# Half of a causal convolution, for the last 2 x 256 tokens, on GpSimd and VectorE instead of TensorE

## The chip, the core and the metric

The kernel runs on one core of a Trainium2 chip. The core has a matrix engine (TensorE, PE in the profile; its weight loads are PEld), three engines for elementwise work (VectorE, DVE; ScalarE, ACT; GpSimd, POOL), and SyncE (SP), which here only issues transfers. Each engine runs its own instructions in the order in which they were issued; between engines, semaphores order the work. TensorE writes only to PSUM, the accumulator memory of eight banks; everything else lies in SBUF, both with 128 partitions. The metric is the device time of one execution in microseconds, median of several runs.

## The reference

The reference computes a retention layer (attention with a fixed decay and no softmax), then a gated linear unit whose gate is a causal convolution of five taps, each channel with its own weights:

```python
scores = q @ k.T / sqrt(64)
x = (scores * gamma[h] ** (i - j), zero for j > i) @ v      # (8, 8, 576, 64) -> (8, 576, 512)
for t in range(5):
    gate_pre += conv_w[t] * xp[:, t:t + 576, :]             # xp: x with four zero tokens in front
out = (sigmoid(gate_pre) * (x @ w_val)) @ w_out
```

Inputs and output are float32; there are 8 batches, 8 heads of 64 channels, and 576 tokens in each batch. The convolution works along the tokens, channel by channel.

## The kernel before

**Units and jobs.** The 576 tokens of a batch are two chunks of 256 and a rest of 64. A chunk is a *unit* of work for the retention; the rests of four batches together make a unit too. There are 18 units: 0 to 15 are chunks, 16 and 17 (`"tail"`) hold the leftover tokens of batches 0 to 3 and 4 to 7, 256 columns each. The gated linear unit works in *jobs*: jobs 0 to 3 are one unit each, jobs 4 to 9 two units, jobs 10 and 11 (`LAST - 1` and `LAST`) are units 16 and 17.

**One unit.** The keys, queries and values are loaded (`load_half`), cast to bf16 (`cast_half`, mostly on GpSimd), turned by TensorE (`turn_bank`), multiplied (`scores`), masked on VectorE (`masks`) and applied to the values, with a carried state for the earlier chunks (`carried`, `values`, `update`, `states`). `take_x` then multiplies the result by the query side of the decay and writes it, bf16, into `xg`. This tile holds x for all tokens as channels (128 partitions x 4 blocks) by tokens, with four zero columns in front of each batch, so that a tap of the convolution is a shifted view of it: `xs(j, rows, blk, shift)`.

**One job.** `conv` does the convolution on TensorE as matmuls with diagonal matrices: `dg` holds, for each block of 128 channels and each tap, a 64x64 diagonal of weights, made from the table `cw` (one column per tap and block) in `prep_conv`. For each pair of blocks (a *set*: blocks 0 and 1, or 2 and 3) it takes 5 taps x 4 quarters = 20 matmuls, and the second block of a set comes out with its two halves of 64 partitions exchanged. `gates` takes the sigmoid of it on ScalarE from PSUM to SBUF (L585; L581 for the last job). `value` is the product with `w_val`, 4 matmuls per block, and `gated` multiplies the two on VectorE into `z` or `zz` (L608). `project` multiplies by `w_out`, for the even and odd tokens of a unit apart (r = 0, 1), ScalarE copies the result into `big` (L623), and `store` sends it out by transfers issued on SP. The last job has its own end: two value products (L940) with their products on VectorE (L941), then `last_rows`, which projects job 11 into the PSUM tiles `s`, `a` and `v`, copies them with ScalarE and VectorE (L638 to L640) and issues the last stores.

**PSUM tiles.** `a`, `s` and the two `o` tiles have one buffer each, `v` has two. A new use of such a tile waits until the last reader of the use before is done. So the order of the readers on ScalarE and VectorE decides when TensorE may go on.

**Order.** There is no planner: the calls in the program are the order on every engine. All work around the change is in the lines behind the loop over the units (L894 to L942): for n = 16 it finishes units 16 and 17, then alternates the convs and value products of jobs 10 and 11 with the projections of units 14, 15 and 16 (`rows_out`), and ends with `last_rows`. Every helper that issues a matmul does so by one wrapper, so all matmuls carry line 169, and the tile names tell them apart: `a<-xg,dg` or `s<-xg,dg` is a conv, `v<-xg,wvb` a value product, `<-wob` a projection.

Of the kernel before, what the change touches and what calls it, by code (L numbers as in the profile page):

```python
# [13 lines left out]
F32 = mybir.dt.float32  # L14
BF16 = mybir.dt.bfloat16
AF = mybir.ActivationFunctionType
ALU = mybir.AluOpType
# [4 lines left out]
def kernel(  # L22
# [10 lines left out]
    nc = tc.nc  # L33
    B, H, S, D = q.shape
    DM = moe_w_val.shape[0]
    KC = moe_conv_w.shape[0]
    P = 128
    NP = H // 2
    NCH = S // P
    TAIL = S - NCH * P  # L40
# [3 lines left out]
    W = 2 * P  # L44
# [7 lines left out]
    ldp = ctx.enter_context(tc.tile_pool(name="ld", bufs=2))  # L52
# [22 lines left out]
    LAST = len(jobs) - 1  # L75
    HALVED = 3
    lo, hi = slice(0, 64), slice(64, 128)
# [3 lines left out]
    with tc.manual_schedule():  # L81
# [52 lines left out]
        taps = moe_conv_w.rearrange("k (o i) -> (k o) i", i=P)  # L134
# [112 lines left out]
        wob = consts.tile([P, NP, DM], BF16, name="wob")  # L247
        dg = consts.tile([P, NP, KC, 64], BF16, name="dg")

        def prep_conv():  # L250
            n = KC * NP
            cps = ps_a.tile([P, 2 * n + 4], F32, name="a")
            twice = cwn.rearrange("p e i -> p (e i)")
            transpose(cps[:, 0:n], twice[:, 0:P], identf[0:n, 0:n])
            transpose(cps[:, n + 1:2 * n + 1], twice[:, 64:192], identf[0:n, 0:n])
            cw = small.tile([P, n], F32, name="cw")
            nc.vector.tensor_copy(cw.rearrange("p (m e) -> p m e", e=2),
                                  cps.rearrange("p (e m two) -> p m e two", e=2, two=2)[:, 0:n // 2, :, 0])
            nc.vector.tensor_tensor(
                dg.rearrange("p o k j -> p k o j"),  # L260
                cw.rearrange("p (k o) -> p k o", o=NP).unsqueeze(3).to_broadcast([P, KC, NP, 64]),
                id2.unsqueeze(1).unsqueeze(1).to_broadcast([P, KC, NP, 64]), op=ALU.mult)
# [69 lines left out]
        def turn_bank(u, hf, ps, take=True):  # L332
            for i in range(2):
                for prl in range(2):
                    for r in range(2):
                        h = 2 * (2 * hf + prl)
                        transpose(ps[:, i, prl, r, :], bf[u]["kq"[i]][:, r, h:h + 2, :].rearrange("p h d -> p (h d)"), ident)
            if take:
                take_bank(u, hf, ps)

        def take_bank(u, hf, ps, eng=None):
            new_turned(u)
            (eng or nc.scalar.copy)(kqt[u][hf].rearrange("p i l r c a -> p (i l r c a)"), ps.rearrange("p i l r a -> p (i l r a)"))  # L343
# [9 lines left out]
        def turn_halves(*pairs, pool=None):  # L353
            if len(pairs) == 1 and pool is None:
                turn_bank(*pairs[0], ps_v.tile([P, 2, 2, 2, P], BF16, name="v"))
            else:
                ps = ps_a.tile([P, 2, 2, 2, 2, P], BF16, name="a")
                for (at, pair) in enumerate(pairs):
                    turn_bank(*pair, ps[:, at], take=False)
                for (at, pair) in enumerate(pairs):  # L360
                    take_bank(*pair, ps[:, at])
# [105 lines left out]
        def take_x(u, cs=(0, 1)):  # L467
            kind, b, cu = units[u]
            x = xg
            o = ops[u]  # L470
            for c in cs:
                if kind == "full":
                    i0 = (2 * cu + c) * P
                    nc.vector.tensor_tensor(  # L474
                        x[:, b, :, PAD + i0:PAD + i0 + P].rearrange("p o (a r) -> p o r a", r=2),
                        o[c].rearrange("p o (r a) -> p o r a", r=2),
                        gout[:, :, i0:i0 + P].rearrange("p o (r a) -> p o r a", r=2), op=ALU.mult)
                else:
                    i0 = NC2 * W
                    for i in range(2):  # L480
                        nc.vector.tensor_tensor(
                            x[:, b + 2 * c + i, :, PAD + i0:PAD + S].rearrange("p o (a r) -> p o r a", r=2),
                            o[c].rearrange("p o (r a) -> p o r a", r=2)[:, :, :, i * 32:i * 32 + 32],
                            gout[:, :, i0:S].rearrange("p o (r a) -> p o r a", r=2), op=ALU.mult)
# [58 lines left out]
        def width(j):  # L543
            return W * len(jobs[j])

        def xs(j, rows, blk, shift):
            kind, b, c = units[jobs[j][0]]
            if kind == "full":
                c0 = c * W + shift
                return xg[rows, b, blk, c0:c0 + width(j)]  # L550
            c0 = NC2 * W + shift
            return xg[rows, b:b + GB * len(jobs[j]), blk, c0:c0 + TAIL]

        gsb, zsb = {}, {}
# [3 lines left out]
        def sets(j, i):  # L558
            return (0, 1) if len(jobs[j]) == 1 and j != HALVED else (i,)

        cps = {}

        def conv(j, i, gate=True, pool=None):
            n, ss = width(j), sets(j, i)
            g = (pool or ps_a).tile([P, 2, 2 * W], F32, name="s" if pool else "a").rearrange("p e (s n) -> p e s n", n=n)[:, :, 0:len(ss)]
            for si, s in enumerate(ss):
                a, b = 2 * s, 2 * s + 1
                for kk in range(KC):
                    for (rows, blk, cols, bank) in ((lo, a, lo, 0), (hi, a, hi, 0), (lo, b, hi, 1), (hi, b, lo, 1)):
                        matmul(g[cols, bank, si, :], lhsT=dg[rows, blk, kk, :], rhs=xs(j, rows, blk, kk),  # L570
                                         start=(si == 0 and kk == 0), stop=(si == len(ss) - 1 and kk == KC - 1),
                                         skip_group_check=True)
            cps[j, i] = g
            if gate:
                gates(j, i)

        def gates(j, i):
            if j == LAST:
                t = [gp.tile([P, 1, len(sets(j, i)), width(j)], F32, name=f"last{e}", bufs=1) for e in range(2)]
                for e in range(2):  # L580
                    nc.scalar.activation(t[e], cps[j, i][:, e:e + 1], AF.Sigmoid)  # L581
                t = [t[e][:, 0] for e in range(2)]
            else:
                t = gp.tile([P, 2, 2 * W], F32, name="gate").rearrange("p e (s n) -> p e s n", n=width(j))[:, :, 0:len(sets(j, i))]
                nc.scalar.activation(t, cps[j, i], AF.Sigmoid)  # L585
                t = [t[:, e] for e in range(2)]
            gsb[j, i] = t
            if i == 0:
                if len(jobs[j]) == 1:
                    zsb[j] = zp.tile([P, NP, width(j)], BF16, name="z", bufs=4)  # L590
                else:
                    zsb[j] = zp.tile([P, NP, width(j)], BF16, name="zz", bufs=2)
# [54 lines left out]
        def stores(n):  # L647
            for u in waiting[:n]:
                store(u)
            del waiting[:n]  # L650

        def store(u):
            kind, b, c = units[u]
            ob = outs[u]
            if kind == "full":
                nc.sync.dma_start(out=out[b, c * W:(c + 1) * W, :].rearrange("(p r) n -> p r n", r=2), in_=ob)
            else:
                for i in range(GB):
                    nc.sync.dma_start(out=out[b + i, NC2 * W:S, :].rearrange("(p r) n -> p r n", r=2),
                                      in_=ob[i * 32:(i + 1) * 32])  # L660
# [3 lines left out]
        def gate_values(j, i, e):  # L664
            value(j, i, e)
            gated(j, i, e)
# [167 lines left out]
        for n in range(4, NU - 2):  # L834
# [4 lines left out]
            j, i = (HALVED, n - 4) if n < 6 else place[n - 2 - n % 2][0:1] + (n % 2,)  # L839
# [54 lines left out]
        n = NU - 2  # L894
        stores(2)
        j = place[n - 1][0]

        def rows_out(u, pools):
            for r in range(2):
                project(*place[u], r, pool=pools[r])  # L900
            waiting.append(u)
            stores(2)
# [10 lines left out]
        scores(n + 1, 0)  # L913
        masks(n + 1, 0)
        turn_halves((n + 1, 1), pool=ps_a)
        rows_out(n - 3, (None, None))
        scores(n + 1, 1, lambda: carried(n + 1, 1), pool=ps_a)
        masks(n + 1, 1)
# [7 lines left out]
        conv(LAST - 1, 0)  # L926
        gated(j, 1, 1)
        take_x(n + 1)
        stores(2)
        rows_out(n - 2, (ps_s, None))  # L930
        gate_values(LAST - 1, 0, 0)
        gate_values(LAST - 1, 0, 1)
        conv(LAST, 0)
        rows_out(n - 1, (ps_s, ps_o))
        gate_values(LAST, 0, 0)
        rows_out(n, (ps_s, ps_o))
        vp = [ps_v.tile([P, W], F32, name="v") for b in range(2)]
        for b in range(2):
# [34 lines left out]
```

## Time and profile before

| | us |
|---|---|
| median of three runs (lowest, highest) | 156.22 (156.05, 157.23) |
| the profiled execution's own time | 156.97 |
| its span, from the first to the last instruction or transfer | 155.3 |
| busy: TensorE / VectorE / ScalarE / GpSimd | 141.3 / 106.3 / 94.5 / 103.2 |
| granted clock of TensorE, mean | 0.999 |

The engines' own times at the end, from the timeline: the tokens of unit 16 are gathered by VectorE at 130.10 to 131.59 us from the start (`take_x`, L481), those of unit 17 at 137.39 to 138.87; the conv of job 10 is on TensorE from 136.68 us on, that of job 11 from 141.51 us; `last_rows` begins at 147.97 and the last copy out of PSUM ends at 150.55. The stores land by 155.3.

Durations in the profile are those of one execution. A "group" in it is all instructions of one line, engine, operation and shape: how many, their busy time, the mean of one in nanoseconds, and how long the engine sat idle before them, with what ended that. "128x512 bf16<-128x512 f32" gives output and input as partitions x elements. The "chain that ended last" goes back from the last instruction to what released it, step by step. "issue" is time in which the engine waited for nothing that the profile shows.

### The profile page before, as it was taken

Reading aid. Unit: us, or ns where it says so; the run is one execution under the profiler, and the core shown is the slowest. Engines: PE = TensorE matmul, PEld = TensorE weight load, DVE = VectorE, ACT = ScalarE, POOL = GpSimd, SP = SyncE. Lnnn points to the kernel's source line nnn. Section 1 sums busy time; section 2 is a strip of 40 time slices with the busy share of each in tenths; the row PEclk is TensorE's granted clock in tenths of the full one; section 3 lists DMA queues with packets and bytes.
Section 4 is the critical chain, followed back from the end, with each engine's and each line's share of the span. In section 5 each row is a group of like instructions: output and inputs, shape, how many; then the busy total and the mean of one; then the engine's idle time right before and its main releaser. Section 6 shows DMA issues by size and latency. Waiting matters only on the chain.

```text
span 155.3 us, 7164 instructions
## 1 busy us (share of the span) xinstructions
PE 141.3 (91%) x3054; PEld 89.9 (58%) x3054; DVE 106.3 (68%) x222; ACT 94.5 (61%) x161; POOL 103.2 (66%) x167
## 2 busy tenths in 40 slices
PE   6877979989698999899999999999999999999960
PEld 2356666878547465656565665647565645557530
DVE  4877785598686568587968796776778678653130
ACT  6995747585676775656567676766665544533530
POOL 7878788879998949794978789697869371000000
PEclk9999999999999999999999999999999999999999
DMA  4999999999999777789878997999979828995355
GB/s 111 347 347 342 313 313 294 332 301 344 275 306 269 209 252 231 223 235 304 258 210 226 303 293 215 283 292 272 214 243 248 231 48 324 412 412 220 133 141 135
DMA packets 62194, 40.60 MB, mean 261 GB/s; under 512 B 3498, under 2 KB 58834, under 8 KB 62162
## 3 DMA queue, kind: packets, MB, share of 16 engines
q1 hardware_dynamic: 61488, 39.59, 83.9%
q10 hardware_dynamic: 674, 0.55, 1.3%
q8 instruction: 24, 0.39, 1.1%
q14 instruction: 8, 0.07, 0.1%
HBM read 30.43 MB, written 9.44 MB: 257 GB/s over the span
## 4 chain that ended last, share of the span: by engine, by line
PE 68%; SPq 10%; DMA 8%; POOL 4%; ACT 3%; issue 3%; DVE 1%; POOLq 0%; ACTq 0%; DVEq 0%
PE v L169 35%; PE a L169 18%; PE s L169 8%; PE o L169 7%; DMA fk<-in_k_dram 5%; SPq L98 4%; DMA fq<-in_moe_w_val_dram 3%; SPq L121 3%; SPq L150 2%; ACT wvb L268 1%; POOL vb L290 1%; ACT gate L585 1%; DVE z L608 1%; POOL qb L297 1%; POOL s L530 0%
## 5 line engine op out<-in xcount | busy, mean ns | idle before, releaser
L169 PE MATMUL v<-xg,wvb 128*128 128x256 bf16 (+1 forms) x192 | 35.2, 326 | 0.2 <-ACT wvb L268 0.2
L343 ACT COPY kq<-a 128x1024 bf16<-128x1024 bf16 x25 | 25.3, 1012 | 16.6 <-PE a L169 15.9
L290 POOL TENSOR_TENSOR vb<-fv,gin 128x512 bf16<-128x512 f32 x32 | 32.7, 1042 | 3.2 <-DMA fv<-in_v_dram 3.2
L608 DVE TENSOR_TENSOR zz<-gate,v 128x512 bf16<-128x512 f32 x24 | 16.5, 687 | 15.1 <-PE v L169 12.4
L585 ACT ACTIVATE gate<-a 128x1024 f32<-128x1024 f32 (+1 forms) x17 | 16.5, 973 | 15.5 <-PE a L169 15.5
L398 DVE TENSOR_TENSOR p<-s,mask 128x1024 bf16<-128x1024 f32 x16 | 19.5, 1220 | 7.8 <-PE s L169 7.8
L169 PEld LDWEIGHTS <-wvb 128*128 128x128 bf16 x192 | 17.6, 97 | 11.8 <-issue 1.0
L474 DVE TENSOR_TENSOR xg<-o,gout 128x512 bf16<-128x512 f32 x32 | 22.3, 737 | 2.2 <-PE o L169 2.2
L169 PE MATMUL a<-xg,dg 64*64 64x256 bf16 (+1 forms) x460 | 21.7, 321 | 0.3 <-DVE xg L474 0.3
L297 POOL CAST kb<-fk 128x512 bf16<-128x512 f32 x32 | 19.7, 617 | 2.6 <-DMA fk<-in_k_dram 2.0
L623 ACT COPY big<-v 128x512 f32<-128x512 f32 x29 | 16.9, 581 | 6.2 <-PE v L169 6.0
L169 PE MATMUL v<-wob,zz 128*128 128x512 bf16 x84 | 20.1, 379 | 0.0
L169 PEld LDWEIGHTS <-kb 64*64 64x64 bf16 (+1 forms) x652 | 14.7, 106 | 8.3 <-DVE p L398 0.9
L297 POOL CAST qb<-fq 128x512 bf16<-128x512 f32 x26 | 15.9, 613 | 3.2 <-DMA fq<-in_q_dram 3.1
L394 DVE TENSOR_TENSOR p<-v,mask 128x512 bf16<-128x512 f32 x26 | 16.7, 683 | 0.5
L169 PEld LDWEIGHTS <-kq 64*64 64x64 bf16 x576 | 11.3, 106 | 9.5 <-issue 8.1
L169 PEld LDWEIGHTS <-dg 64*64 64x64 bf16 x480 | 12.8, 106 | 4.6 <-issue 0.7
L169 PEld LDWEIGHTS <-zz 128*128 128x128 bf16 x96 | 8.8, 98 | 9.5 <-issue 0.7
L169 PE MATMUL o<-p,vb 64*64 64x128 bf16 x576 | 13.1, 218 | 0.8 <-issue 0.4
L169 PE MATMUL o<-kq,s 64*64 64x128 bf16 (+1 forms) x256 | 11.2, 212 | 0.6 <-issue 0.5
L169 PEld LDWEIGHTS <-vb 64*64 64x64 bf16 x576 | 10.0, 107 | 2.5 <-issue 2.4
L608 DVE TENSOR_TENSOR z<-gate,v 128x512 bf16<-128x512 f32 (+1 forms) x12 | 7.0, 589 | 6.0 <-PE v L169 5.8
(108 smaller groups left out, 210.5 us busy)
## 6 DMA issues: line engine op xcount, KB each, us to landing
out_dram<-big SPq DMA_DIRECT2D x16, 512.0 KB, 5.9
fk<-in_k_dram SPq DMA_DIRECT2D x28, 256.0 KB, 4.7
fq<-in_q_dram SPq DMA_DIRECT2D x28, 256.0 KB, 4.8
fv<-in_v_dram SPq DMA_DIRECT2D x27, 256.0 KB, 4.6
big<-in_k_dram SPq DMA_DIRECT2D x2, 512.0 KB, 5.0
big<-in_q_dram SPq DMA_DIRECT2D x2, 512.0 KB, 5.5
big<-in_v_dram SPq DMA_DIRECT2D x2, 512.0 KB, 5.9
big<-in_moe_w_out_dram SPq DMA_DIRECT2D x4, 256.0 KB, 4.8
```

What stands on the lines that cost most here:

```text
L98: nc.sync.dma_start(out=t, in_=src[b, :, c * W:(c + 1) * W, :].rearrange("h (p r) d -> p h (r d)", r=2))
L121: queue.dma_start(out=t[:, hs], in_=SRC[n][b, hs, c * W:(c + 1) * W, :].rearrange("h (p r) d -> p h (r d)", r=2))
L169: return f(*a, **k)
L290: nc.gpsimd.tensor_tensor(b[n][:, hs].rearrange("p h r d -> p (h r) d"), f.rearrange("p h (r d) -> p (h r) d", r=2), gin[:, units[u][2], h ...
L297: (eng or nc.gpsimd.tensor_copy)(b[n][:, :, hs].rearrange("p r h d -> p h r d"), f.rearrange("p h (r d) -> p h r d", r=2))
L343: (eng or nc.scalar.copy)(kqt[u][hf].rearrange("p i l r c a -> p (i l r c a)"), ps.rearrange("p i l r a -> p (i l r a)"))
L394: nc.vector.tensor_tensor(p[:, par].rearrange("p l r a -> p l (r a)"), sps[u, hf][par].rearrange("p l r a -> p l (r a)"), mrow.to_broadcas ...
L398: nc.vector.tensor_tensor(p.rearrange("p e l r a -> p (e l) (r a)"), sps[u, hf].rearrange("p e l r a -> p (e l) (r a)"), mrow.to_broadcast ...
L474: nc.vector.tensor_tensor(x[:, b, :, PAD + i0:PAD + i0 + P].rearrange("p o (a r) -> p o r a", r=2), o[c].rearrange("p o (r a) -> p o r a", ...
L585: nc.scalar.activation(t, cps[j, i], AF.Sigmoid)
L608: nc.vector.tensor_tensor(zsb[j][:, 2 * e + ss[0]:2 * e + ss[-1] + 1, :], gsb[j, i][e], vps[j, i, e], op=ALU.mult)
L623: (eng or nc.scalar.copy)(outs[u][:, r], o)
```

## The change

For jobs 10 and 11 alone, TensorE's `conv` does only the first set (blocks 0 and 1). Blocks 2 and 3 are computed from the same `xg` by a new function, `conv_off`, in float32:

- Block 2 on GpSimd. Five instructions multiply the shifted views by their column of `cw`, the first into the job's sum, the others into four parts of a scratch tile; three additions bring these together.
- Block 3 on VectorE. One such product, then four instructions that each multiply a view by its weight and add it to the sum.

The sums lie in one tile (`fq`, four parts of 256 columns: two jobs, two blocks) and the scratch in another (`fk`); these are the buffers into which queries and keys were loaded before. `gates_off` takes the sigmoid of the sums on ScalarE, from SBUF, into the second half of the gate tiles. For block 3 it is two instructions, which exchange the halves of 64 partitions as the matmuls did. The sigmoids that read PSUM take only the first set.

In the order of the calls, GpSimd's part for job 10 stands right after the turning of unit 17; VectorE's for job 10 and GpSimd's for job 11 after `take_x` of unit 17; VectorE's for job 11 after the last product of job 10 with its gate. Matmuls of `value`, `project` and `last_rows` stay as they are.

```diff
+            taken.append(cw)                                   # in prep_conv
...
+        OFF = (LAST - 1, LAST)
+
+        def conv_off(j, e, eng):
+            if not pre:
+                free = [ldp.tile([P, H, 2 * D], F32, name=nm).rearrange("p h d -> p (h d)").rearrange("p (t n) -> p t n", n=W)
+                        for nm in ("fk", "fq")]
+                for at, jj in enumerate(OFF):
+                    pre[jj] = free[1][:, 2 * at:2 * at + 2]
+                pre["taps"] = free[0]
+            acc = pre[j][:, e]
+            for kk in range(KC):
+                w = taken[0][:, kk * NP + 2 + e:kk * NP + 3 + e]
+                x = xs(j, slice(0, P), 2 + e, kk)
+                if eng is nc.vector and kk > 0:
+                    a = acc.rearrange("p (g n) -> p g n", n=TAIL)
+                    eng.scalar_tensor_tensor(out=a, in0=x, scalar=w, in1=a, op0=ALU.mult, op1=ALU.add)
+                else:
+                    t = acc if kk == 0 else pre["taps"][:, kk - 1]
+                    eng.tensor_scalar(out=t.rearrange("p (g n) -> p g n", n=TAIL), in0=x, scalar1=w, scalar2=None, op0=ALU.mult)
+            if eng is not nc.vector:
+                t = pre["taps"]
+                eng.tensor_tensor(t[:, 0:2], t[:, 0:2], t[:, 2:4], op=ALU.add)
+                eng.tensor_tensor(t[:, 0], t[:, 0], t[:, 1], op=ALU.add)
+                eng.tensor_tensor(acc, acc, t[:, 0], op=ALU.add)
+
+        def gates_off(j, e):
+            t = gsb[j, 0][e]
+            if e == 0:
+                nc.scalar.activation(t[:, 1], pre[j][:, 0], AF.Sigmoid)
+            else:
+                for (a, b) in ((lo, hi), (hi, lo)):
+                    nc.scalar.activation(t[a, 1], pre[j][b, 1], AF.Sigmoid)
 
         def conv(j, i, gate=True, pool=None):
-            n, ss = width(j), sets(j, i)
+            n, ss = width(j), sets(j, i)[0:1] if j in OFF else sets(j, i)
...
-                    nc.scalar.activation(t[e], cps[j, i][:, e:e + 1], AF.Sigmoid)
+                    nc.scalar.activation(t[e][:, :, 0:1], cps[j, i][:, e:e + 1], AF.Sigmoid)
...
-                nc.scalar.activation(t, cps[j, i], AF.Sigmoid)
+                nc.scalar.activation(t[:, :, 0:1] if j in OFF else t, cps[j, i], AF.Sigmoid)
...
         turn_halves((n + 1, 1), pool=ps_a)
+        conv_off(LAST - 1, 0, nc.gpsimd)
...
         take_x(n + 1)
+        conv_off(LAST - 1, 1, nc.vector)
+        conv_off(LAST, 0, nc.gpsimd)
+        gates_off(LAST - 1, 0)
         stores(2)
         rows_out(n - 2, (ps_s, None))
         gate_values(LAST - 1, 0, 0)
+        gates_off(LAST - 1, 1)
         gate_values(LAST - 1, 0, 1)
+        conv_off(LAST, 1, nc.vector)
         conv(LAST, 0)
         rows_out(n - 1, (ps_s, ps_o))
+        gates_off(LAST, 0)
         gate_values(LAST, 0, 0)
+        gates_off(LAST, 1)
         rows_out(n, (ps_s, ps_o))
```

More of the change, by code (lines that the diff above doesn't have):

```diff
@@ L248 @@
         dg = consts.tile([P, NP, KC, 64], BF16, name="dg")
+        taken = []
         def prep_conv():
@@ L559, in sets @@
             return (0, 1) if len(jobs[j]) == 1 and j != HALVED else (i,)
-        cps = {}
+        cps, pre = {}, {}
+        OFF = (LAST - 1, LAST)
[28 more added lines that the diff above has]
+                    nc.scalar.activation(t[a, 1], pre[j][b, 1], AF.Sigmoid)
         def conv(j, i, gate=True, pool=None):
-            n, ss = width(j), sets(j, i)
+            n, ss = width(j), sets(j, i)[0:1] if j in OFF else sets(j, i)
             g = (pool or ps_a).tile([P, 2, 2 * W], F32, name="s" if pool else "a").rearrange("p e (s n) -> p e s n", n=n)[:, :, 0:len(ss)]
```

## The prediction

> **What bounds the kernel now.** I read the page first, then the chain of work that ended last in order of time, then the timeline of every engine from 126 us on, because the change touches only the end of the kernel.
>
> ```profile
> span 155.3 us, 7164 instructions
> ...
> PE 141.3 (91%) x3054; PEld 89.9 (58%) x3054; DVE 106.3 (68%) x222; ACT 94.5 (61%) x161; POOL 103.2 (66%) x167
> ...
> POOL 7878788879998949794978789697869371000000
> ```
>
> TensorE is busy 91% of the span. GpSimd's slices are empty after about 128 us: that is the idle engine the change uses.
>
> ```profile
> 136.75 1.24 PE a L169 x40
> 137.99 0.97 PE s L169 x4
> 138.96 2.62 PE v L169 x20
> 141.58 1.24 PE a L169 x40
> ...
> 146.39 0.86 PE o L169 x4
> 147.26 0.88 PE v L169 x8
> 148.14 0.43 PE s L169 x2
> ...
> 149.69 0.57 ACT big L638
> ```
>
> The columns are start, us and engine; from 129.35 to 149.67 us this chain is TensorE alone, without a gap. The two pieces of 40 matmuls into `a` are the convs of the two leftover-token jobs, 10 and 11: 1.24 us each, 31 ns a matmul. So a matmul removed there is time removed, if TensorE waits for nothing new.
>
> **What is removed.** Half of both convs: 2 x 20 x 31 ns = 1.24 us of TensorE. All that is issued behind moves up 0.62 us, then 1.24 us: the value product of job 11 from 144.5 to 143.3, `last_rows` from 147.97 to 146.73. The sigmoids halve too (L585 1.02 to about 0.58 us), off the path. That is 0.8% of the time, so no reading of the change gives a gain over 1%; 1% (1.56 us) is about what a measurement of this kernel can tell from no change.
>
> **What is added, and the rows for its prices.** From the groups of instructions by line and shape (count | busy us, mean ns of one | idle before):
>
> ```profile
> L529 POOL TENSOR_TENSOR mid<-run,xf 128x256 f32<-128x256 f32 x8 | 5.8, 725 | 7.7 <-ACT xf L508 6.8 <-ACT xf L506 0.8
> ...
> L530 POOL CAST s<-mid 128x256 bf16<-128x256 f32 x8 | 3.2, 396 | 0.5
> ```
>
> GpSimd, per job: five scaled copies of 128x256 (one tensor input and a scalar column), one add of 128x512, two of 128x256. A scaled copy is in no row. The bounds are the cast of the same size, 0.40 us (one input), and the add, 0.73 us (two inputs); I take 0.40, since it reads one tensor. The 128x512 add: casts of 256 and 512 elements (0.396 and 0.617) leave 0.175 fixed, so (0.725 - 0.175) x 2 + 0.175 = 1.27 us (bounds 1.04, the `vb` product, and 1.45, two small adds). Dependent GpSimd steps stand 0.06 us apart. Sum: 5 x 0.37 (independent ones overlap by 0.03) + 1.27 + 2 x 0.73 + 3 x 0.06 = 4.8 us; with 0.73 for a copy 6.4.
> The Trainium skill (GPSIMD Engine Reference, Engine selection) says that one-input work on GpSimd is roughly at line rate and two-input work about twice as slow as VectorE; by it a copy is priced like the cast, as I took it, and the sum would not change.
>
> VectorE, per job: one scaled copy and four fused multiply-adds, all from SBUF, each needing the one before. No row has the fused form. Two VectorE sums with both inputs in SBUF give 0.206 us for 64 elements (L193) and 1.491 for 1280 (L259), so 0.41 for 256. Lower bound 0.41; upper bound 0.69, the `zz` product of twice the size; I take 0.45, because the scalar is read from memory as well, and 0.04 between dependent steps (L218 to L219): 0.49 a step, 2.45 us for five.
>
> ScalarE: sigmoids from SBUF, one of 128x256 and two of 64x256 per job. The 128x256 copy out of PSUM takes 0.38 (L640); from SBUF the 512-element casts take 0.04 more than the copies, so 0.41, and 0.75 for the pair.
>
> **The collision.** The trace has one VectorE sum of exactly this kind beside a busy GpSimd. The timeline of each engine (start us, duration us):
>
> ```profile
> 43.65 1.36 DVE L474 TENSOR_TENSOR xg<-o,gout 128x512 bf16<-128x512 f32 x2
> ...
> 44.98 1.04 DVE L540 TENSOR_TENSOR s<-mid,xf 128x256 bf16<-128x256 f32 x1
> ```
> ```profile
> 43.69 2.04 POOL L290 TENSOR_TENSOR vb<-fv,gin 128x512 bf16<-128x512 f32 x2
> 45.68 0.80 POOL L297 CAST kb<-fk 128x512 bf16<-128x512 f32 x1
> 46.43 0.61 POOL L297 CAST qb<-fq 128x512 bf16<-128x512 f32 x1
> ```
>
> It took 1.04 us instead of 0.41: it ended 0.29 us after the `vb` product in front of it on GpSimd (45.73), and GpSimd's next cast took 0.80 instead of 0.61. The L474 product just before, with one input in PSUM, kept its usual 0.7. So two-input SBUF work on VectorE waits out the GpSimd instruction that runs, and then GpSimd waits. The Trainium skill (SBUF — State Buffer, Terms, on the shared port pair) says that this pair is an exclusive lock which VectorE or GpSimd holds for a full instruction, so that the other blocks fully. It speaks against this change; the 1.04 us row agrees that the wait is long, the 0.80 us cast (0.19 late, not 0.41) that some of it overlaps, and by full blocking the sum would be the 157.3 us of the upper bound below.
>
> **The sum, along the timeline.** Job 10 on GpSimd can start when the gathering of its tokens ends (L481, 131.59). VectorE runs nothing with two SBUF inputs until 137.4. It ends at 131.65 + 4.8 = 136.5 (138.1 by the high price). Its sigmoid is behind the halved one, at 138.07, ahead of the copies of unit 14. Cover: 1.6 us. No cost.
>
> Next both engines wait for the same event, the end of L481 at 138.87. VectorE then does job 10's other block while GpSimd starts job 11's. First step to 139.32; the other four alternate with GpSimd's copies: after the collided step above, GpSimd ended 0.46 later with a 512-element cast, 0.22 less for 256, then 0.29 + 0.04 for the step, so about 0.6 us a pair. (Bounds: 0.49, no collision; 0.40 + 0.45 = 0.85, nothing overlapped, which puts all that follows 1 us later: 157.3 us.) End 139.32 + 4 x 0.6 = 141.7. Queued behind it on VectorE: job 10's products with the gates. On ScalarE: the pair of sigmoids, 141.8 to 142.5, ahead of job 11's gates. The products end at 142.4 and 143.3. TensorE needs their PSUM buffers at 143.4 and 146.0 and their result at 144.3: covered, by 1 us at the least.
>
> Then VectorE starts its block of job 11 at 143.3, between its other work and the two small adds of GpSimd (copies done at 142.0, big add to 143.3, small ones to 144.1 and 144.85). 2.45 us of its own plus two waits, 0.55 and 0.4: end 146.6. GpSimd ends at about 145.2; its sigmoid is done by 145.7. But on ScalarE the other pair waits for 146.6, and the copies of unit 16 wait behind it: pair to 147.4, first copy to 147.98 (0.58), and only then is the `s` bank free for `last_rows`: 148.03. VectorE meanwhile multiplies job 11 (146.6 to 147.3), which frees the `v` buffer for the last value product, done at 147.8.
>
> So `last_rows` starts at 148.03 against 147.97 now: 0.06 us later. TensorE's 1.24 us become waiting. What follows (1.72 us of matmuls, the copies, the store's flight) is unchanged; unit 16's four store issues on SP (1.74 us from 148.6) end just before the last ones at 150.6. The profiled execution took 156.97 us around its span of 155.3, so it would take 157.0; on the median of the runs, 156.22, **156.3 us**. The all-low end (0.41 a step, no collision) is TensorE's full 1.24: 155.0.
>
> **Rivals.**
> 1. *TensorE stays the bound.* If VectorE's block of job 11 ends by 145.3, `last_rows` starts at 146.73: 155.0 us. For it: without collisions at 0.45 a step (0.41 and 0.04) the two blocks end at 141.1 and about 144.9. Against it: the 1.04 us row. Chance 0.12.
> 2. *GpSimd's scaled copy is dear*, the slower side. At 0.73 us a copy a pair costs 0.70 + 0.29 = 0.99: VectorE's first block ends at 143.3, products and sigmoids at 144.85, the second block at 148.2, `last_rows` at 149.63: 1.66 us late, 157.9 us. Each 0.1 us on the copy costs 0.4 us; at 0.40 the gain is just used up, from about 0.7 on it is over 1%. For it: no row has a scalar column on GpSimd. Against it: one input, as the cast. A VectorE step of 0.6 us would act alike (10 steps, +0.15 each). Chance 0.24.
> 3. *GpSimd keeps the port through its chain*, so that VectorE's four steps wait until 143.7 and end at 145.6; products and sigmoids at 147.1, second block 149.55, `last_rows` 151.0: 3 us late, 159.2. Against it: in the lines above VectorE came in between two GpSimd instructions that stood back to back. Chance 0.08.
> 4. *The four sums lie in one tile* and are run one after another, so the engines don't work side by side: GpSimd's job 11 starts at 141.3, ends 146.1, VectorE's last block 148.5: `last_rows` 149.95, 2 us late, 158.2. Against it: at 123.85 TensorE read three blocks of `zz` while VectorE still wrote the fourth, so parts of a tile are waited for singly. Chance 0.06.
>
> **How the numbers follow.** My forecast, with 0.3 us either side, holds the rest, 0.50. Over 1% slower: rivals 3 and 4, and about 0.16 of rival 2's 0.24, with a few more for other new waits: 0.31. Over 1% faster: 0.02, for the scatter of the runs. Within 1%: 0.67. The range takes in rival 1 below and rivals 2 and 4 above: 155.0 to 158.6.
>
> **What would show it.** Conv pieces of 20 matmuls, 0.62 us each. GpSimd copies at 0.40, VectorE steps at 0.45 alone and over 0.6 while GpSimd works. A wait of TensorE, in the chain, for ScalarE's copy of unit 16 or VectorE's product just before `last_rows`; if the chain stays all TensorE to the end, rival 1 holds. Dearer copies, or steps bunched behind GpSimd's last add, would make it wrong upward.

## The result, and the profile after

The changed kernel takes 157.99 us (median), the kernel before, run beside it, 156.04: a ratio of 1.011, 95% interval 1.008 to 1.014, so 1.2 to 2.2 us slower. The forecast was 156.3 us within 155.0 to 158.6. The time lies in the range, but the forecast saw next to no change, and the loss is real: the range held it only because its upper side had been drawn for rivals 2 and 4. The forecast itself, with its 0.3 us either side, ended at 156.6.

The profiled execution of the changed kernel took 158.11 us, its span is 156.4. First the page (busy us, share, instructions; GpSimd's row of 40 slices):

```profile
span 156.4 us, 7122 instructions
...
PE 140.6 (90%) x3014; PEld 88.6 (57%) x3014; DVE 111.8 (71%) x232; ACT 96.1 (61%) x167; POOL 118.3 (76%) x183
...
POOL 7779688567899979796986979697786273999500
```

TensorE does 40 instructions less. GpSimd, which was empty after 128 us, is busy from 131.4 to 147.2: 15.1 us more work, where 2 x 4.8 had been reckoned. Next the chain that ended last, in order of time (start us, us, what):

```profile
131.39 0.94 POOL fq L583
132.33 3.61 POOL fk L583 x4
...
138.90 0.94 POOL fq L583
139.83 4.14 POOL fk L583 x4
...
144.05 1.40 POOL fk L586
...
145.52 0.79 POOL fk L587
...
147.64 0.41 ACT last L596
...
148.51 0.59 ACT big L658
...
149.15 0.59 PE s L169 x2
```

Before, this stretch was TensorE alone. Now it is GpSimd from 131.4 to 147.2, then ScalarE, and only then `last_rows`. The scaled copies (L583) are the greatest part of it. GpSimd's timeline (start, duration) shows, for the first job, what one of them costs, and that the additions cost what was reckoned:

```profile
131.39 0.94 POOL L583 TENSOR_SCALAR fq<-xg,cw 128x256 f32<-128x256 bf16 x1 [3.19 <-DVE xg L484]
132.31 3.62 POOL L583 TENSOR_SCALAR fk<-xg,cw 128x256 f32<-128x256 bf16 x4
136.01 1.27 POOL L586 TENSOR_TENSOR fk<-fk 128x512 f32<-128x512 f32 x1
137.36 0.73 POOL L587 TENSOR_TENSOR fk<-fk 128x256 f32<-128x256 f32 x1
138.17 0.72 POOL L588 TENSOR_TENSOR fq<-fq,fk 128x256 f32<-128x256 f32 x1
```

A scaled copy takes 0.94 us, not 0.40; the four behind it take 0.90 each from start to start. And TensorE's timeline has two gaps that were not there before:

```profile
140.36 1.04 PE L169 MATMUL v<-xg,wvb 128*128 128x256 bf16 x8 [0.59 <-ACT big L658]
141.33 0.75 PE L169 MATMUL a<-xg,dg 64*64 64x256 bf16 x20
...
148.39 0.60 PE L169 MATMUL v<-xg,wvb 128*128 128x256 bf16 x4 [1.44 <-DVE z L643]
149.15 0.59 PE L169 MATMUL s<-wob,z 128*128 128x512 bf16 x2
```

The first is job 10: GpSimd's sum is ready at 138.89, its sigmoid stands on ScalarE ahead of unit 14's copies, and TensorE stands idle for 0.59 us until the copy that frees a `v` buffer. The second is job 11: GpSimd's sum is ready at 147.17, its sigmoid at 147.62, the product with the gate at 148.34, and only then is a `v` buffer free for the last value product (148.39). What ends last is on ScalarE, as the chain shows: the pair of sigmoids stands behind GpSimd's sigmoid, the copy of unit 16 behind the pair, and its end at 149.10 frees the `s` bank for `last_rows`. VectorE's sum, for which the pair also waits, had been ready since 146.59. The conv of 20 matmuls is there too.

Since the first 130 us differ a little from one execution to the next, the runs below are compared within the stage, from the end of `take_x` of unit 17 (VectorE, four products into `xg`, 138.87 us before) to the start of `last_rows`. What follows `last_rows` is the same in all. Before: 147.97 - 138.87 = 9.10 us. After: 149.15 - 138.51 = 10.64, 1.54 more, which fits the measured ratio.

### The profile page after: what moved, and what is told of

Read it like the earlier page. It is cut to its first block, busy times and chain, and to the rows that moved or that the text cites. A ratio compares the mean times of both kernels' runs of the same rounds, so it can differ in the third digit from the quotient of the medians.

```text
span 156.4 us, 7122 instructions
## 1 busy us (share of the span) xinstructions
PE 140.6 (90%) x3014; PEld 88.6 (57%) x3014; DVE 111.8 (71%) x232; ACT 96.1 (61%) x167; POOL 118.3 (76%) x183
## 4 chain that ended last, share of the span: by engine, by line
PE 61%; POOL 10%; DMA 10%; DVE 8%; ACT 4%; issue 2%; SPq 1%; POOLq 1%; ACTq 0%; DVEq 0%
PE v L169 32%; PE a L169 16%; PE o L169 7%; PE s L169 6%; POOL fk L583 5%; DMA fk<-in_k_dram 4%; DMA big<-in_q_dram 3%; DVE p L401 3%; DMA fq<-in_q_dram 2%; POOL fk L586 2%; ACT gate L620 1%; DVE p L397 1%; POOL fq L583 1%; DVE xg L477 1%; POOL fk L587 1%
## 5 line engine op out<-in xcount | busy, mean ns | idle before, releaser
L169 PE MATMUL a<-xg,dg 64*64 64x512 bf16 (+1 forms) x420 | 20.6, 326 | 0.3 <-DVE xg L477 0.3
L169 PEld LDWEIGHTS <-dg 64*64 64x64 bf16 x440 | 11.7, 106 | 4.9 <-issue 1.1
L532 POOL TENSOR_TENSOR mid<-run,xf 128x256 f32<-128x256 f32 x8 | 5.8, 725 | 7.0 <-ACT xf L511 4.2
```

The source lines that it names most:

```text
L169: return f(*a, **k)
L532: nc.gpsimd.tensor_tensor(mids[u], state[b, "run"], xf[:, 0], op=ALU.add)
```

## The experiments

**Theory A**: GpSimd's scaled copy is dear, and GpSimd's chain sets the end. **Theory B**: the collisions of VectorE and GpSimd set it. **Theory C**: VectorE's chain with the sigmoids behind it sets it by itself. All times in this table are us from the end of `take_x` of unit 17, in the profiled execution; the columns of GpSimd and VectorE are of job 11, and a dash means that the engine does nothing of it. The ratio is that of the whole time to the kernel before.

| run | GpSimd's last sum | VectorE's last step | `last_rows` starts | ratio (95% interval) |
|---|---|---|---|---|
| before | - | - | 9.10 | 1 |
| the change | 8.66 | 8.08 | 10.64 | 1.011 (1.008 to 1.014) |
| e1 GpSimd's blocks only | 7.84 | - | 9.50 | 1.0016 (0.9985 to 1.0048) |
| e2 VectorE's blocks only | - | 6.25 | 9.09 | 1.0005 (0.9968 to 1.0042) |
| e3 products, not scaled copies | 6.73 | 8.05 | 9.59 | 1.0028 (0.9993 to 1.0063) |
| e5 five casts, no sums | 2.62 | 6.31 | 7.99 | 0.9898 (0.9849 to 0.9947) |
| e6 job 10 only | - | - | 8.55 | 0.9986 (0.9961 to 1.0011) |
| e7 job 11 only, on VectorE | - | 6.08 | 8.54 | 0.9995 (0.9965 to 1.0025) |
| e8 three products on ScalarE | 5.51 | 7.36 | 8.45 | 0.9988 (0.9961 to 1.0015) |
| e9 e3 with another order | 6.73 | 8.05 | 9.14 | 1.0005 (0.9968 to 1.0041) |
| e10 spread over three engines | 6.00 | 4.61 | 8.75 | 0.9962 (0.9924 to 1.0001) |

### One engine's part alone (e1, e2)

```diff
 # conv, in the loop over the quarters of a pair of blocks
+    if si == 1 and bank in OFF.get(j, ()):     # e1: OFF = {10: (0,), 11: (0,)}
+        continue                               # e2: OFF = {10: (1,), 11: (1,)}
```

> Only block 2 of both jobs leaves TensorE (GpSimd); block 3 stays a conv on TensorE, so no VectorE step runs beside GpSimd. Theory A (the price of GpSimd's scaled copy: 0.93 us where 0.40 was reckoned, so GpSimd's chain sets the end): the copies stay at 0.93, the chain of the last job ends about 0.8 us earlier than in the changed kernel for lack of collisions (7.5 us instead of 8.3), one sigmoid, one copy of unit 16 and last_rows follow: about 0.5 us slower than before, 156.5. Theory B (the collisions of VectorE and GpSimd set the end): without them TensorE keeps its 0.62 us: 155.4. A copy that falls to 0.40 here would be the end of A.

> Only block 3 of both jobs leaves TensorE (VectorE); block 2 stays a conv on TensorE, GpSimd is idle at the end. Theory A: VectorE's five steps take 0.35 + 4 x 0.49 without GpSimd beside them, both blocks are done before 145 us, TensorE stays the bound and keeps its 0.62 us: 155.4. Theory B gives the same here. Theory C (VectorE's chain with the pair of sigmoids behind it sets the end by itself): about 1 us slower than before, 157.

In e1 the copies stay at 0.93 us and GpSimd's last sum comes 0.8 us earlier than in the change, as A said; `last_rows` is 0.40 us later than before, TensorE having waited for GpSimd alone. But the 0.62 us that both expectations granted TensorE do not exist. e2 shows it best, since nothing waits in it; its chain in order of time:

```profile
134.86 1.23 PE a L169 x30
136.09 0.97 PE s L169 x4
137.06 2.62 PE v L169 x20
139.68 1.23 PE a L169 x30
```

Thirty matmuls take 1.23 us, as forty did (1.24), while twenty take 0.68 in the change (141.33 to 142.01). The matmuls of one tap, four quarters of a pair of blocks, cost the same when two of the four are left out, as they would if the four ran beside each other. So half a pair gains nothing. With that corrected, e2 is what "VectorE costs nothing, TensorE gains nothing" gives (9.09 against 9.10), and C falls: VectorE's last step ends at 6.25, far ahead of `last_rows`. e1 speaks for A, since it has no VectorE step to collide with and is late all the same.

### The same sums without the scaled copy (e3), and what makes it dear (e4)

```diff
 # shortened: the views of t are left out
-    eng.tensor_scalar(out=t, in0=x, scalar1=w, scalar2=None, op0=ALU.mult)            # on GpSimd
+    eng.tensor_tensor(t, x, w.unsqueeze(2).to_broadcast([P, GB, TAIL]), op=ALU.mult)
```

> As the changed kernel, but GpSimd's scaled copies are products of two tensors, the second being the weight's column spread over the row. Theory A: the vb products with such a column take 1.04 for 512 elements, so about 0.6 (up to 0.73) for 256; GpSimd's first chain ends near 137.5, the second at 145.3 to 146 instead of 147.2, and last_rows 2.0 us behind it: between 0.2 us faster and 0.4 slower than before, about 156.2. Theory B: products of two tensors hold the port for longer than the scaled copies did, VectorE's steps wait more, and the time stays at 158 or rises.

> Prices only: of GpSimd's five scaled copies of each job four are replaced by another form (so the sums are not the convolution): the second by a copy with a fixed factor, the third by a plain cast of the same view, the fourth by a scaled copy of 256 contiguous float32 elements, the fifth by a product with the spread column. If the scalar column makes the copy dear: fixed factor and cast 0.40, contiguous float32 0.93, product about 0.6. If the bf16 input or the shifted view of 4 x 64 makes it dear: contiguous float32 0.40, the fixed factor and the cast 0.93, the product above 0.9.

The prices, from GpSimd's timeline of e4 (one execution), in the first chain, where VectorE does no step of the convolution beside it:

```profile
131.09 0.94 POOL L597 TENSOR_SCALAR fq<-xg,cw 128x256 f32<-128x256 bf16 x1 [3.10 <-DVE xg L484]
132.00 0.85 POOL L586 TENSOR_SCALAR fk<-xg 128x256 f32<-128x256 bf16 x1
132.79 0.40 POOL L589 CAST fk<-xg 128x256 f32<-128x256 bf16 x1
133.16 0.93 POOL L592 TENSOR_SCALAR fk<-gout,cw 128x256 f32<-128x256 f32 x1
134.06 0.62 POOL L595 TENSOR_TENSOR fk<-xg,cw 128x256 f32<-128x256 bf16 x1
```

Both explanations in the expectation fall. A fixed factor in place of the column saves 0.09 us; contiguous float32 in place of the shifted bf16 view 0.01. A cast of the very same view takes 0.40, and a product of two tensors, which reads more, 0.62. So neither the view nor the column is dear by itself; it is the scaled copy that is slow on GpSimd. Why it is, no run here shows, nor whether one with a fixed factor on contiguous float32, which was not tried, would be cheap.

e3 uses that: GpSimd's last sum comes 1.93 us earlier, and of the 1.54 us lost 1.05 come back. That is A's main proof. The rest is not the price of the copy: now VectorE is last.

```profile
138.93 0.31 DVE L586 TENSOR_SCALAR fq<-xg,cw 128x256 f32<-128x256 bf16 x1
139.28 2.98 DVE L580 SCALAR_TENSOR_TENSOR fq<-xg,cw,fq 128x256 f32<-128x256 bf16 x4
142.19 0.67 DVE L646 TENSOR_TENSOR z<-gate,v 128x512 bf16<-128x512 f32 x1
143.17 0.69 DVE L646 TENSOR_TENSOR z<-gate,v 128x512 bf16<-128x512 f32 x1 [0.31 <-ACT gate L599]
143.78 0.46 DVE L586 TENSOR_SCALAR fq<-xg,cw 128x256 f32<-128x256 bf16 x1
144.27 2.81 DVE L580 SCALAR_TENSOR_TENSOR fq<-xg,cw,fq 128x256 f32<-128x256 bf16 x4
```

This is VectorE's timeline of e3. Four fused steps take 2.98 and 2.81 us here; alone, in e2, they take 2.05 both times. So B is right about a part: with cheap copies, the collisions decide.

### What TensorE's gain is worth when nothing holds it (e5)

```diff
 # shortened
-    eng.tensor_scalar(...)                # GpSimd: five scaled copies and three additions
+    eng.tensor_copy(acc, x)               # five casts, no additions
```

> As the changed kernel, but GpSimd only casts the five views (0.40 us each) and leaves the weights and the additions out, so that its part of the convolution is missing. Theory A (the price of GpSimd's chain took TensorE's gain): with a chain of about 2 us TensorE waits for nothing and the whole 1.24 us shows, 1.0 to 1.2 us faster than before. If less than half of it shows, something else than GpSimd holds the end, VectorE's chain or the order of the sigmoids.

GpSimd's timeline of e5, then its chain that ended last:

```profile
138.36 2.56 POOL L584 CAST fq<-xg 128x256 f32<-128x256 bf16 x5 [5.62 <-DVE xg L484]
```
```profile
140.46 0.68 PE a L169 x20
...
145.58 0.88 PE v L169 x8
146.46 0.43 PE s L169 x2
```

`last_rows` starts 1.11 us earlier than before, and the whole time is lower by 1.0% (0.5 to 1.5). VectorE does its two blocks as in the change, and the chain is TensorE to the end. So the gain exists in full, no other wait hides it, and all of the loss comes from GpSimd's part, with the collisions that it makes for VectorE (whose last step ends at 6.31 here, at 8.08 in the change). It is 1.11 and not 1.24 because twenty matmuls take 0.68 us, not half of 1.24: 2 x (1.24 - 0.68) = 1.12.

### One job alone (e6, e7)

```diff
 # e6
-        OFF = (LAST - 1, LAST)
+        OFF = {LAST - 1: (0, 1)}          # with e3's products on GpSimd
 # e7
+        OFF = {LAST: (0, 1)}              # both blocks: conv_off(LAST, e, nc.vector)
```

> Only job 10 gives its half away (GpSimd as products with the spread column, VectorE by taps); job 11 stays on TensorE. Theory A: GpSimd's chain for job 10 ends at about 137.5, ahead of the halved sigmoid, VectorE's five steps run alone after 138.9 and end at 141.2; nothing waits, TensorE keeps 0.62 us of one conv: 0.6 us faster than before. If job 10's part has a cost of its own, less than 0.3.

> Only job 11 gives its half away, both blocks to VectorE (2 x 2.4 us from 138.9 on, around job 10's products); GpSimd does nothing. No collision, second block done at about 145.1, pair of sigmoids at 146.0, the first copy of unit 16 at 146.6, last_rows at 147.35 instead of 147.97: 0.6 us faster than before. Theory C (VectorE's chain and the sigmoids behind it set the end): last_rows later than 147.97, no gain.

In the stage both do what was expected: 0.55 and 0.56 us earlier, TensorE without a wait. In the whole time neither can be told from the kernel before; both intervals reach down to about 0.996, where 0.56 us would lie. So each job's half can be given away at no cost, by itself: job 10's, for which GpSimd has the tokens seven microseconds earlier, and job 11's when VectorE alone has it. The two together do not fit as the change lays them out.

### Other distributions (e8, e9, e10)

```diff
 # e9: e3, and
-        gates_off(LAST, 1)
         rows_out(n, (ps_s, ps_o))
+        gates_off(LAST, 1)
 # e8: e9, and for job 11, block 2
-        conv_off(LAST, 0, nc.gpsimd)
+        conv_off(LAST, 0, nc.gpsimd, (0, 1))
+        scalar_taps(LAST, 0, (2, 3, 4))   # nc.scalar.activation(tap, x, AF.Copy, scale=w), behind unit 14's copies
+        sums(LAST, 0)                     # GpSimd's three additions
 # e10, in words: e9, and job 10's block 3 on GpSimd too, taps 1 to 4 of both block 2 on ScalarE, job 11's block 3 alone on VectorE
```

> As the run with products of the spread column, and the pair of sigmoids of job 11 stands behind the two copies of unit 16 on ScalarE instead of ahead of them. If the order of ScalarE is what is left of the loss there: last_rows waits for the last value product alone and begins about 0.4 us earlier, 9.2 us behind the gathering of unit 17 instead of 9.6, level with the kernel before (9.1). If VectorE's second block is (its end frees the buffer of the last value product), less than 0.2 us.

> Both jobs as in the change, GpSimd with products of the spread column, but three of job 11's five products of block 2 move to ScalarE (scaled copies, about 0.41 us each, behind unit 14's copies), and the pair of sigmoids of job 11 stands behind unit 16's copies. GpSimd's chain for job 11 ends at about 144.2, VectorE's second block at about 145.9, last value product at 147.1, last_rows there: about 0.8 us faster than before. If collisions cost more than reckoned, VectorE's block ends after 146.7 and the gain is nil.

> The same two halves leave TensorE, spread otherwise: job 10's block 3 goes to GpSimd too, eight of the ten products of block 2 go to ScalarE (0.42 us each, in its idle time), VectorE has only job 11's block 3. GpSimd's chain for job 11 ends about 6.2 us behind the gathering of unit 17, the last product with its gate at 7.4, last_rows at about 8.0 to 8.2 us behind it, where the kernel before has 9.1: 0.9 to 1.1 us faster than before. If ScalarE or VectorE's collisions with GpSimd hold it, over 8.5 and no more than 0.6 us.

e9 moves only the pair of sigmoids and wins 0.45 us against e3: the copy of unit 16 behind them had held `last_rows`, as the forecast had it. What is left is VectorE's second block, whose end frees the last `v` buffer. e8 shortens GpSimd's chain and comes to 8.45: 0.65 us earlier than before where about 0.8 was expected, and short of the 7.99 that is to be had, with VectorE's second block (7.36) still last. e10 was expected at 8.0 to 8.2 and came to 8.75: GpSimd's two-tensor instructions, additions but for one product, fill the time in which VectorE does its block (five steps from 138.87 to 143.39, 4.5 us), job 10's products with the gate wait behind it, and TensorE waits 0.62 us for them:

```profile
142.39 1.03 PE L169 MATMUL o<-wob,zz 128*128 128x512 bf16 x4
144.04 1.04 PE L169 MATMUL v<-xg,wvb 128*128 128x256 bf16 x8 [0.62 <-DVE z L659]
```

No version that computes the whole convolution is faster than the kernel before beyond the uncertainty of the runs. e10 comes nearest by the whole time (0.9962, up to 1.0001), e8 by the stage; all of e6 to e10 are faster than the change.

## Why the prediction was right or wrong

- **What bounds the kernel** (TensorE, in the stage of the change): right. e5 shows the gain once nothing new holds it.
- **What is removed**, 1.24 us: a tenth too much. Half of a conv saves 0.56, not 0.62 (e5, and the conv pieces).
- **GpSimd's scaled copy, taken at 0.40 us with bounds of 0.40 and 0.73: this is the step that failed.** It takes 0.93, beyond even the dearer bound. "One tensor input, so it is priced like the cast" was the wrong reason: the number of inputs does not set it, since the product of two tensors takes 0.62. Ten copies at 0.53 more are 5.3 us of GpSimd's chain. The trace of before had a nearer row than the cast: the `vb` products (L290) multiply by spread columns too, as products of two tensors, at 1.04 us for 512 elements. The Trainium skill (GPSIMD Engine Reference, Engine selection) calls one-input work on GpSimd roughly line-rate; here one such rate does not serve for both, the cast with 0.40 us and the scaled copy with 0.93.
- **Additions** 1.27 and 0.73, **sigmoids** 0.41: right to 0.01 us (measured 1.27, 0.72 to 0.73, 0.42). The pair was taken at 0.75 and takes 0.84, as the two do not overlap.
- **VectorE's steps** at 0.49 each: right. Alone, four take 2.05 us (0.51 each), the first of a block 0.35.
- **The cover of job 10** (1.6 us, "no cost"): gone with the price. GpSimd's sum is ready 0.38 us after the end of `take_x` of unit 17 instead of 2.4 before it, and TensorE stands idle for 0.59.
- **The collision**, 0.6 us a pair: right in kind, and its size depends on what runs beside it. Between two-tensor products a step takes 0.75 (e3), beside the scaled copies only 0.55 (the change), alone 0.51.
- **What is late next**: the forecast named VectorE's second block, and behind it the pair of sigmoids, the copy of unit 16 and the `s` bank. The end of this path is right: TensorE does wait for that copy just before `last_rows`. Its head is not: in the change GpSimd's sum comes 0.58 us after VectorE's and holds the pair. With cheaper copies it is as forecast: e3 has VectorE's last step at 8.05 where the forecast had 7.7 (146.6 - 138.9), and `last_rows` 0.49 late where it had 0.06. The 0.43 between them are about 0.35 of collisions more and the dearer pair.
- **Rival 2** (dear copies) is what happened, at a chance of 0.24, and its time, 157.9, is nearly the measured one. Yet its path was another. It let VectorE wait out each dear copy, 0.99 us a pair. VectorE does not: it is GpSimd's own end, 8.66, that is late, and then its sigmoid, the pair and the copy of unit 16. The agreement of the times is luck: by rival 2's own 0.4 us for each 0.1 us on the copy, 0.93 instead of 0.73 adds 0.8 us, which gives 158.7. **Rival 3** falls: VectorE comes in between GpSimd's instructions everywhere. **Rival 4** falls too: both engines write parts of one tile side by side. **Rival 1** (TensorE stays the bound) did not happen in the change; e5 shows its gain, 1.11, with GpSimd's chain cut short.

## What to carry to other kernels

An operation that the trace of before does not show on an engine has no upper bound from its neighbours there: price it by a run of its own, or ask what happens at three times the price and put the chance there. When work leaves the engine that bounds a stage, its replacement has to be done by the same deadline, and the last piece, whose input comes latest, decides; give away the early piece first. Before counting removed instructions as time, see which of them run beside each other: the half that is left may take as long as the whole.

## What the runs showed of the hardware

- GpSimd, 128x256 to float32: cast 0.40 us, product with a spread column 0.62, sum of two float32 tensors 0.73, scaled copy 0.93 with a column as factor, whether from a shifted bf16 view or contiguous float32, and 0.85 with a fixed one from the view. A multiplication by a column is cheaper there as a product of two tensors.
- VectorE's fused multiply-add with both tensors in SBUF does not wait for the whole of a scaled copy on GpSimd: it starts every 0.55 us beside copies of 0.93, two of which in turn grow to about 1.15. Beside two-tensor instructions it waits until the running one ends: in e3, and beside the additions here, such a step ends about 0.3 us after a GpSimd instruction does. VectorE's timeline of the change has the one, then the other:

```profile
139.08 2.23 DVE L580 SCALAR_TENSOR_TENSOR fq<-xg,cw,fq 128x256 f32<-128x256 bf16 x4
...
143.21 3.38 DVE L580 SCALAR_TENSOR_TENSOR fq<-xg,cw,fq 128x256 f32<-128x256 bf16 x4
```

The first four steps fall on scaled copies (2.23 us). Of the second four (3.38), the first two begin beside the last scaled copy (0.58 and 0.48), the other two fall on the additions (1.37 while the 128x512 addition runs, then 0.84). Alone, four take 2.05. The Trainium skill (SBUF — State Buffer, Terms) has the loser blocked for a full instruction; the additions agree, the scaled copies do not.
- Quarter matmuls (64x64) of 256 columns: 40 take 1.24 us, 30 take 1.23, 20 take 0.68. Here only whole groups of four quarters saved time.
